# Clustered attention with two feed-forward layers: two instructions that fold the attention output are moved within a hand-written order

## The chip, the cores and the metric

The kernel runs on one core of a Trainium2 chip. The metric is the device time of one execution in microseconds (us); before the change the median of three runs is 757.99 us. Engines are named as in the profile: PE (TensorE matmul), PEld (its weight loads), DVE (VectorE), ACT (ScalarE), POOL (GpSimd) and SP (SyncE, which issues all DMAs here).

## The reference, cut to what matters

Sixteen heads (2 batches of 8) of 768 rows and 64 columns go through attention in which a row sees only the columns of its own cluster; the cluster of a row is the centroid with the largest product. Two dense layers follow, on 1536 rows.

```python
q_assign = argmax(q_n @ c_n.T); k_assign = argmax(k_n @ c_n.T)
scores = where(q_assign[:, None] == k_assign[None, :], q @ k.T / 8, -1e9)
attn = exp(scores - max(scores)); attn = attn / (sum(attn) + 1e-9)
x = attn @ v                                  # heads side by side: 1536 x 512
h = x @ w_in;  x = maximum(0.01 * h, h) @ w_out
h = x @ w_in2; x = maximum(h, 0) ** 2 @ w_out2
```

## The kernel before, in words

Attention takes the first third of the time. It works on 8 pairs of heads, each pair in 6 **units** (3 for each head) of 256 query rows, 48 units in all. A unit u is taken through a pipeline several steps deep; the loop at L712 makes step after step, and in each step it issues the operations that one string of `PLAN` (L21 to L46) lists, in that order. `X0:0` in step u means the first exponential of unit u, `Va:3` means part a of the product with v of unit u-3, `S1:-1` the second score tile of unit u+1. An item with `@` belongs to the preparation of the next pair. Step s below is the step that uses string s, so steps 0 to 5 make up a pair. The order of each engine is exactly the order of the strings (`manual_schedule`, L524) for PE, DVE, ACT and POOL, up to unit 41; from step 42 on (L718) a planner that works from estimated costs and priorities places the instructions of these four engines, until the feed-forward part takes up a hand-written order again. SP's order is always that of the program.

The operations of one unit, with their engine:

- S0, S1 (PE, L389): scores of 128 rows each into a PSUM tile S; two such tiles exist, one for the even and one for the odd half. In steps 5 and 0 some of them also carry the cluster products of the next pair (L297) in the rest of the tile.
- R0, R1 (DVE, L412): row maximum of S. X0, X1 (ACT, L422): exponential of S, with the row sums.
- RE (ACT, L433) adds a small constant to the two row sums; RC (DVE, L436) takes their reciprocal; N0, N1 (POOL, L439) multiply the exponentials by it.
- Ta, Tb, Tc (PE, L452): transposes into a PSUM tile T, of which three exist. Ha, Hb, Hc (ACT, L463) and La, Lb, Lc (DVE, L469) copy T out as a high and a low part, eh and el.
- Va, Vb, Vc (PE, L487): products of eh and el with v, accumulated in the PSUM tile A, of which one exists. Va of a unit therefore needs the unit before to be out of A.
- **FC** (ACT, `fold_a`, L500) copies one half of A's partitions into xt; **FA** (DVE, `fold_b`, L509) adds the other half to it. So FA needs FC, and FC needs Vc.

The preparation of the next pair that matters here: M0, M1 and M2 (DVE, L318 and L319) read the cluster products out of the S tiles in step 0. Then come `desc` (POOL, L324), `m2` (DVE, L330, one reduction in step 1), `oh` (POOL, L337 and L339, the one-hot rows, issued in step 2 ahead of N0 and N1), and `oT` (PE, L350, three transposes of the one-hot rows, step 2 behind Vc). They run so for the pairs 2 to 7, that is six times; the first two pairs are prepared otherwise. `FIRST` selects the same six strings for the first pair.

In both kernels an order list says what each engine does; what an instruction waits for is derived from the tiles, in the order of the program.

```python
    def fold_a(u):
        ...
        nc.scalar.copy(
            out=xt_t[p][64 * j : 64 * j + 64, c : c + 256], in_=a_t[u][64 - 64 * j : 128 - 64 * j]
        )
    def fold_b(u):
        ...
        nc.vector.tensor_tensor(out=x, in0=a_t.pop(u)[64 * j : 64 * j + 64], in1=x, op=ALU.add)
```

Of the kernel before, what the change touches and what calls it, by code (L numbers as in the profile page):

```python
# [19 lines left out]

PLAN = (  # L21
    (
        "ldq@0 Ta:2 X0:0 FA:4 RC:1 Va:3 khi@0 Hc:3 M0@0 Ha:2 R1:0 M1@0 Lc:3 S0:-1 Tb:2 X1:0 "
        "Vb:3 Hb:2 La:2 RE:0 Vc:3 klo@0 N0:1 R0:-1 M2@0 Lb:2 N1:1 S1:-1 FC:3 Tc:2"
    ),
    (
        "Ta:2 qhi@0 qlo@0 X0:0 FA:4 RC:1 Va:3 Hc:3 Ha:2 desc@0 R1:0 Lc:3 S0:-1 Tb:2 X1:0 "
        "Vb:3 Hb:2 La:2 RE:0 Vc:3 N0:1 R0:-1 Lb:2 m2@0 N1:1 S1:-1 FC:3 Tc:2"
    ),
    (  # L30
        "Ta:2 X0:0 FA:4 pl00@0 RC:1 Va:3 Hc:3 oh@0 Ha:2 R1:0 Lc:3 S0:-1 Tb:2 X1:0 Vb:3 "
        "pl10@0 Hb:2 La:2 RE:0 Vc:3 oT@0 N0:1 R0:-1 Lb:2 N1:1 S1:-1 FC:3 Tc:2"
    ),
    (
        "Ta:2 X0:0 FA:4 RC:1 st@0 Va:3 Hc:3 Ha:2 R1:0 Lc:3 S0:-1 Tb:2 X1:0 Vb:3 "
        "pl01@0 Hb:2 vhi@0 La:2 RE:0 Vc:3 N0:1 R0:-1 Lb:2 xhi@0 N1:1 S1:-1 FC:3 Tc:2"
    ),
    (
        "Ta:2 X0:0 FA:4 RC:1 Va:3 xlo@0 Hc:3 Ha:2 R1:0 Lc:3 S0:-1 Tb:2 X1:0 Vb:3 Hb:2 La:2 "
        "RE:0 Vc:3 N0:1 R0:-1 Lb:2 N1:1 S1:-1 FC:3 Tc:2"  # L40
    ),
    (
        "Ta:2 X0:0 FA:4 RC:1 scale@1 vlo@0 ldv@0 Va:3 Hc:3 Ha:2 R1:0 Lc:3 S0:-1 Tb:2 X1:0 "
        "Vb:3 Hb:2 pl11@0 La:2 RE:0 Vc:3 N0:1 R0:-1 Lb:2 N1:1 S1:-1 FC:3 Tc:2"
    ),
)  # L46
FILL = (0,0,1)
# [1114 lines left out]
```

## Time and profile before

| | |
|---|---|
| median of 3 runs | 757.99 us (757.71 to 758.62) |
| the profiled execution's own time | 756.92 us |
| its span in the profile | 755.1 us |
| busy: PE, PEld, DVE, ACT, POOL | 98%, 86%, 76%, 59%, 51% of the span |
| granted TensorE clock | full in all 40 slices of the span |
| DMA | 66.35 MB, mean 88 GB/s |

The span is what the trace covers, from its first to its last instruction; 1.8 us of the execution lie around it. Busy shares are means over an attention part and a feed-forward part that look different: in the attention part DVE, ACT and POOL are nearly as full as PE. A busy PE is one that has a matmul in flight. In the timelines below each row gives a start, a duration, the engine, the source line, the operation and, in brackets, how long the engine stood idle before it and what ended that.

### The profile page before, as it was taken

To read this page: it belongs to the slowest core of one execution; us is meant where nothing else is said; L and a number is where in the kernel's file an instruction comes from. 1 tells how busy PE (TensorE), PEld (TensorE's weight loads), DVE (VectorE), ACT (ScalarE), POOL (GpSimd) and SP (SyncE) were. 2 spreads that over 40 slices of the span, in tenths; PEclk is the share of its full clock that TensorE was granted. 3 is DMA by queue.
4 is the path that set the end of the run, shared out by engine and by line. 5 is a ranking of instruction groups with operands and counts; after the bars stand their busy time and mean duration, and the time that the engine had idled before them with its cause. 6 is when DMAs were issued, how large, how long until landed. Compare 5 with 4: busy or idle time off the path is not lost.

```text
span 755.1 us, 11072 instructions
## 1 busy us (share of the span) xinstructions
PE 743.5 (98%) x4054; PEld 647.8 (86%) x4054; DVE 573.5 (76%) x860; ACT 442.1 (59%) x816; POOL 387.1 (51%) x345
## 2 busy tenths in 40 slices
PE   8999999999999999999999999999999999999997
PEld 8899999999989888888888888888788888888886
DVE  5999999999999545776666566686868677686755
ACT  6988988988998564345353354547644345444430
POOL 2989889889855316461432414399342341423400
PEclk9999999999999999999999999999999999999999
DMA  7493573572601213111131111311112211121004
GB/s 232 106 224 107 116 176 109 116 173 68 151 27 61 109 56 112 56 56 57 56 112 56 56 56 56 111 57 56 56 57 77 90 57 56 56 89 79 1 1 167
DMA packets 16903, 66.35 MB, mean 88 GB/s; under 512 B 3153, under 2 KB 4049, under 8 KB 11857
## 3 DMA queue, kind: packets, MB, share of 16 engines
q1 hardware_dynamic: 16848, 65.65, 29.2%
q8 instruction: 32, 0.52, 0.3%
q14 instruction: 23, 0.18, 0.1%
HBM read 44.60 MB, written 3.15 MB: 63 GB/s over the span
## 4 chain that ended last, share of the span: by engine, by line
PE 83%; DVE 11%; ACT 5%; issue 1%; POOL 0%; DVEq 0%; ACTq 0%; POOLq 0%
PE o L848 34%; PE h L770 31%; PE A L487 6%; PE S L389 5%; PE T L452 5%; DVE el L469 3%; DVE nm L412 3%; ACT e L422 2%; DVE xt L509 1%; ACT eh L463 1%; DVE xl L1008 1%; DVE ds L319 1%; DVE m L318 1%; PE warm L242 1%; PE S L297 1%
## 5 line engine op out<-in xcount | busy, mean ns | idle before, releaser
L134 POOL TENSOR_TENSOR wl<-wt,wh 128x1024 fp32r<-128x1024 f32 x32 | 76.9, 2403 | 130.7 <-ACT wh L133 130.7
L819 DVE TENSOR_TENSOR gl<-h,gh 128x512 fp32r<-128x512 f32 x96 | 65.7, 690 | 68.9 <-ACT h L814 50.2
L770 PE MATMUL h<-xl,wh 128*128 128x512 f32 x288 | 112.2, 390 | 0.0
L770 PE MATMUL h<-xh,wh 128*128 128x512 f32 x288 | 111.8, 390 | 0.1
L770 PE MATMUL h<-xh,wl 128*128 128x512 f32 x288 | 111.9, 389 | 0.0
L866 DVE TENSOR_TENSOR acc<-o,acc 128x512 f32<-128x512 f32 x144 | 92.9, 686 | 12.4 <-PE o L848 12.4
L469 DVE TENSOR_TENSOR el<-T,eh 128x512 fp32r<-128x512 f32 x144 | 94.4, 683 | 4.4 <-ACT eh L463 3.2
L439 POOL TENSOR_SCALAR e<-e,r 128x768 f32<-128x768 f32 x96 | 87.4, 922 | 18.3 <-DVE r L436 12.1
L412 DVE TENSOR_REDUCE nm<-S 128x1 f32<-128x768 f32 x96 | 90.9, 948 | 4.7 <-PE S L297 2.4
L422 ACT ACTIVATE e<-S,nm 128x768 f32<-128x768 f32 x96 | 87.2, 909 | 11.0 <-DVE nm L412 6.8
L389 PE MATMUL S<-hb 128*128 128x384 f32 (+1 forms) x384 | 90.2, 349 | 1.6 <-ACT e L422 1.2
L463 ACT CAST eh<-T 128x512 fp32r<-128x512 f32 x144 | 79.8, 589 | 13.5 <-PE T L452 13.2
L487 PE MATMUL A<-eh,vv 128*128 128x256 f32 x288 | 79.6, 306 | 2.0 <-DVE xt L509 2.0
L452 PE MATMUL T<-ident,e 128*128 128x128 f32 x576 | 79.6, 273 | 1.0 <-DVE el L469 1.0
L848 PE MATMUL o<-gl,wh 128*128 128x512 f32 x192 | 74.8, 390 | 0.0
L197 POOL TENSOR_TENSOR ws<-wt 128x256 f32<-128x256 f32 x24 | 17.8, 740 | 111.1 <-DVE wt L173 111.1
L848 PE MATMUL o<-gh,wl 128*128 128x512 f32 x192 | 74.7, 389 | 0.0
L848 PE MATMUL o<-wh,gh 128*128 128x512 f32 x192 | 74.7, 389 | 0.0
L848 PE MATMUL o<-wh,gl 128*128 128x512 f32 x192 | 74.7, 389 | 0.0
L848 PE MATMUL o<-wl,gh 128*128 128x512 f32 x192 | 74.7, 389 | 0.0
L848 PE MATMUL o<-gh,wh 128*128 128x512 f32 x192 | 73.6, 389 | 0.0
L487 PE MATMUL A<-el,vv 128*128 128x256 f32 x288 | 72.5, 282 | 0.3 <-DVE el L469 0.3
(136 smaller groups left out, 1600.9 us busy)
## 6 DMA issues: line engine op xcount, KB each, us to landing
wraw<-w SPq DMA_DIRECT2D x32, 1024.0 KB, 4.7
hb<-spl SPq DMA_DIRECT2D x14, 576.0 KB, 4.6
hb<-spl SPq DMA_DIRECT2D x42, 192.0 KB, 5.1
rqk<-qk SPq DMA_DIRECT2D x16, 384.0 KB, 3.8
rv<-v SPq DMA_DIRECT2D x8, 384.0 KB, 3.3
out<-q SPq DMA_DIRECT2D x12, 256.0 KB, 2.0
twice<-qk SPq DMA_DIRECT2D x8, 192.0 KB, 5.9
hb<-st SPq DMA_DIRECT2D x56, 24.0 KB, 1.9
```

Of the source, the lines that this page charges most:

```text
L134: return lambda: nc.gpsimd.tensor_tensor(out=wl, in0=t, in1=wh.bitcast(F32), op=ALU.subtract)
L389: nc.tensor.matmul(out=s[:, c, 0:HALF], lhsT=hb[0:k, a, i * 128 : (i + 1) * 128], rhs=hb[0:k, b, c * HALF : (c + 1) * HALF], start=(a == 0 ...
L412: nc.vector.tensor_reduce(out=n, in_=s_t[t][:, :, 0:HALF], axis=AX.XY, op=ALU.max, negate=True)
L422: nc.scalar.activation(out=e.rearrange("p (a b) -> p a b", a=2), in_=s_t.pop(t)[:, :, 0:HALF], func=AF.Exp, bias=n_t.pop(t), scale=1.0, ac ...
L439: nc.gpsimd.tensor_scalar(out=e_t[t], in0=e_t[t], scalar1=r_t[t // 2][:, t % 2 : t % 2 + 1], scalar2=1.0, op0=ALU.mult, op1=ALU.mult,)
L452: nc.tensor.transpose(T[:, o : o + 128], e_t[2 * u + b][:, kc * 128 : (kc + 1) * 128], ident)
L463: nc.scalar.copy(out=eh[:, 2 * g : 2 * g + 2, :].rearrange("p a b -> p (a b)"), in_=T_t[u, g])
L469: nc.vector.tensor_tensor(out=el[:, 2 * g : 2 * g + 2, :].rearrange("p a b -> p (a b)"), in0=T_t.pop((u, g)), in1=eh[:, 2 * g : 2 * g + 2, ...
L487: nc.tensor.matmul(out=A, lhsT=w, rhs=m[:, kc, :], start=(kc == 0 and i == 0), stop=(kc == KC - 1 and i == 1),)
L770: nc.tensor.matmul(out=out, lhsT=l, rhs=r, start=(first and i == 0), stop=(i == n - 1), skip_group_check=not first,)
L848: nc.tensor.matmul(out=outs[o], lhsT=l, rhs=r, start=(first and i == 0), stop=(last and i == 2),)
L866: nc.vector.tensor_tensor(out=a, in0=ps, in1=a, op=ALU.add)
```

## The change

Only `PLAN` changes, in the same way in its six strings. FC goes from behind S1 to right behind Vc. FA was the second DVE instruction of the step after (lag 4); it becomes lag 3, behind R0 and ahead of Lb. RC goes from behind FA (lag 1) to right behind R0 of its own step (lag 0), ahead of FA. In string 0 this pair of instructions comes ahead of M2 as well. Two of the six strings:

```diff
-        "ldq@0 Ta:2 X0:0 FA:4 RC:1 Va:3 khi@0 Hc:3 M0@0 Ha:2 R1:0 M1@0 Lc:3 S0:-1 Tb:2 X1:0 "
-        "Vb:3 Hb:2 La:2 RE:0 Vc:3 klo@0 N0:1 R0:-1 M2@0 Lb:2 N1:1 S1:-1 FC:3 Tc:2"
+        "ldq@0 Ta:2 X0:0 Va:3 khi@0 Hc:3 M0@0 Ha:2 R1:0 M1@0 Lc:3 S0:-1 Tb:2 X1:0 "
+        "Vb:3 Hb:2 La:2 RE:0 Vc:3 FC:3 klo@0 N0:1 R0:-1 RC:0 FA:3 M2@0 Lb:2 N1:1 S1:-1 Tc:2"
...
-        "Ta:2 qhi@0 qlo@0 X0:0 FA:4 RC:1 Va:3 Hc:3 Ha:2 desc@0 R1:0 Lc:3 S0:-1 Tb:2 X1:0 "
-        "Vb:3 Hb:2 La:2 RE:0 Vc:3 N0:1 R0:-1 Lb:2 m2@0 N1:1 S1:-1 FC:3 Tc:2"
+        "Ta:2 qhi@0 qlo@0 X0:0 Va:3 Hc:3 Ha:2 desc@0 R1:0 Lc:3 S0:-1 Tb:2 X1:0 "
+        "Vb:3 Hb:2 La:2 RE:0 Vc:3 FC:3 N0:1 R0:-1 RC:0 FA:3 Lb:2 m2@0 N1:1 S1:-1 Tc:2"
```

## Rows read from the trace of the kernel before

**Rows 1.** Page: the span, and PE's busy time, share and instructions.

```profile
span 755.1 us, 11072 instructions
...
PE 743.5 (98%) x4054; PEld 647.8 (86%) x4054; DVE 573.5 (76%) x860; ACT 442.1 (59%) x816; POOL 387.1 (51%) x345
```

**Rows 2.** Busy time of each engine in one pair, from step 2 to step 2.

```profile
137.79:166.19 28.40, 28.06 (x220) 27.43 (x220) 26.82 (x50) 24.50 (x57) 25.29 (x25) 1.00 0.55 133
```

**Rows 3.** Waits of PE's weight loads, 14 to 262 us: total, times, longest.

```profile
PEld A L487 <- DVE xt L509: 3.5, 6, 0.6
...
PEld T L452 <- POOL e L439: 1.3, 1, 1.3
```

**Rows 4.** Timeline of DVE, steps 4 to 1 of a pair, up to step 2.

```profile
148.30 0.95 DVE L412 TENSOR_REDUCE nm<-S 128x1 f32<-128x768 f32 x1
...
155.65 0.29 DVE L318 TENSOR_REDUCE m<-S 128x8 f32<-128x128 f32 x1 [0.53 <-ACT e L422]
...
158.84 0.95 DVE L412 TENSOR_REDUCE nm<-S 128x1 f32<-128x768 f32 x1
159.70 0.28 DVE L318 TENSOR_REDUCE m<-S 128x8 f32<-128x128 f32 x1
160.02 0.29 DVE L319 TENSOR_TENSOR ds<-S,m 128x128 f32<-128x128 f32 x1
160.23 0.68 DVE L469 TENSOR_TENSOR el<-T,eh 128x512 fp32r<-128x512 f32 x1
...
161.60 0.96 DVE L412 TENSOR_REDUCE nm<-S 128x1 f32<-128x768 f32 x1
...
164.53 0.68 DVE L469 TENSOR_TENSOR el<-T,eh 128x512 fp32r<-128x512 f32 x1
165.13 0.55 DVE L330 TENSOR_REDUCE m<-ds 128x24 f32<-128x384 f32 x1
165.71 0.43 DVE L509 TENSOR_TENSOR xt<-A,xt 64x256 f32<-64x256 f32 x1
```

**Rows 5.** Timeline of ACT, steps 4, 0 and 1.

```profile
149.23 0.37 ACT L500 COPY xt<-A 64x256 f32<-64x256 f32 x1
...
157.82 0.90 ACT L422 ACTIVATE e<-S,nm 128x768 f32<-128x768 f32 x1 [0.52 <-DVE ds L319]
...
159.61 0.30 ACT L433 ACTIVATE r<-r,eps 128x2 f32<-128x2 f32 x1
160.08 0.36 ACT L500 COPY xt<-A 64x256 f32<-64x256 f32 x1 [0.17 <-PE A L487]
160.47 0.90 ACT L422 ACTIVATE e<-S,nm 128x768 f32<-128x768 f32 x1
...
162.65 0.90 ACT L422 ACTIVATE e<-S,nm 128x768 f32<-128x768 f32 x1 [0.23 <-DVE nm L412]
...
164.33 0.36 ACT L500 COPY xt<-A 64x256 f32<-64x256 f32 x1
```

**Rows 6.** Timeline of PE, steps 1 and 2.

```profile
162.00 0.88 PE L389 MATMUL S<-hb 128*128 128x384 f32 x4
...
164.81 1.04 PE L452 MATMUL T<-ident,e 128*128 128x128 f32 x8
166.19 0.39 PE L487 MATMUL A<-eh,vv 128*128 128x256 f32 x1 [0.34 <-DVE xt L509]
...
168.87 0.34 PE L350 MATMUL ohT<-identb,oh 128*128 128x128 bf16 x3
...
169.82 1.04 PE L452 MATMUL T<-ident,e 128*128 128x128 f32 x8
170.61 0.36 PE L487 MATMUL A<-eh,vv 128*128 128x256 f32 x1
```

**Rows 7.** Timeline of POOL, step 2: one-hot rows, then N0 and N1.

```profile
166.69 1.49 POOL L339 TENSOR_SCALAR oh<-ds 128x384 bf16<-128x384 f32 x1
168.16 1.79 POOL L439 TENSOR_SCALAR e<-e,r 128x768 f32<-128x768 f32 x2
```

More of the change, by code (lines that the diff above doesn't have):

```diff
@@ L22 @@
     (
-        "ldq@0 Ta:2 X0:0 FA:4 RC:1 Va:3 khi@0 Hc:3 M0@0 Ha:2 R1:0 M1@0 Lc:3 S0:-1 Tb:2 X1:0 "
-        "Vb:3 Hb:2 La:2 RE:0 Vc:3 klo@0 N0:1 R0:-1 M2@0 Lb:2 N1:1 S1:-1 FC:3 Tc:2"
-    ),
-    (
-        "Ta:2 qhi@0 qlo@0 X0:0 FA:4 RC:1 Va:3 Hc:3 Ha:2 desc@0 R1:0 Lc:3 S0:-1 Tb:2 X1:0 "
-        "Vb:3 Hb:2 La:2 RE:0 Vc:3 N0:1 R0:-1 Lb:2 m2@0 N1:1 S1:-1 FC:3 Tc:2"
-    ),
-    (
-        "Ta:2 X0:0 FA:4 pl00@0 RC:1 Va:3 Hc:3 oh@0 Ha:2 R1:0 Lc:3 S0:-1 Tb:2 X1:0 Vb:3 "
-        "pl10@0 Hb:2 La:2 RE:0 Vc:3 oT@0 N0:1 R0:-1 Lb:2 N1:1 S1:-1 FC:3 Tc:2"
-    ),
-    (
-        "Ta:2 X0:0 FA:4 RC:1 st@0 Va:3 Hc:3 Ha:2 R1:0 Lc:3 S0:-1 Tb:2 X1:0 Vb:3 "
-        "pl01@0 Hb:2 vhi@0 La:2 RE:0 Vc:3 N0:1 R0:-1 Lb:2 xhi@0 N1:1 S1:-1 FC:3 Tc:2"
-    ),
-    (
-        "Ta:2 X0:0 FA:4 RC:1 Va:3 xlo@0 Hc:3 Ha:2 R1:0 Lc:3 S0:-1 Tb:2 X1:0 Vb:3 Hb:2 La:2 "
-        "RE:0 Vc:3 N0:1 R0:-1 Lb:2 N1:1 S1:-1 FC:3 Tc:2"
-    ),
-    (
-        "Ta:2 X0:0 FA:4 RC:1 scale@1 vlo@0 ldv@0 Va:3 Hc:3 Ha:2 R1:0 Lc:3 S0:-1 Tb:2 X1:0 "
-        "Vb:3 Hb:2 pl11@0 La:2 RE:0 Vc:3 N0:1 R0:-1 Lb:2 N1:1 S1:-1 FC:3 Tc:2"
+        "ldq@0 Ta:2 X0:0 Va:3 khi@0 Hc:3 M0@0 Ha:2 R1:0 M1@0 Lc:3 S0:-1 Tb:2 X1:0 "
+        "Vb:3 Hb:2 La:2 RE:0 Vc:3 FC:3 klo@0 N0:1 R0:-1 RC:0 FA:3 M2@0 Lb:2 N1:1 S1:-1 Tc:2"
+    ),
+    (
+        "Ta:2 qhi@0 qlo@0 X0:0 Va:3 Hc:3 Ha:2 desc@0 R1:0 Lc:3 S0:-1 Tb:2 X1:0 "
+        "Vb:3 Hb:2 La:2 RE:0 Vc:3 FC:3 N0:1 R0:-1 RC:0 FA:3 Lb:2 m2@0 N1:1 S1:-1 Tc:2"
+    ),
+    (
+        "Ta:2 X0:0 pl00@0 Va:3 Hc:3 oh@0 Ha:2 R1:0 Lc:3 S0:-1 Tb:2 X1:0 Vb:3 "
+        "pl10@0 Hb:2 La:2 RE:0 Vc:3 FC:3 oT@0 N0:1 R0:-1 RC:0 FA:3 Lb:2 N1:1 S1:-1 Tc:2"
+    ),
+    (
+        "Ta:2 X0:0 st@0 Va:3 Hc:3 Ha:2 R1:0 Lc:3 S0:-1 Tb:2 X1:0 Vb:3 "
+        "pl01@0 Hb:2 vhi@0 La:2 RE:0 Vc:3 FC:3 N0:1 R0:-1 RC:0 FA:3 Lb:2 xhi@0 N1:1 S1:-1 Tc:2"
+    ),
+    (
+        "Ta:2 X0:0 Va:3 xlo@0 Hc:3 Ha:2 R1:0 Lc:3 S0:-1 Tb:2 X1:0 Vb:3 Hb:2 La:2 "
+        "RE:0 Vc:3 FC:3 N0:1 R0:-1 RC:0 FA:3 Lb:2 N1:1 S1:-1 Tc:2"
+    ),
+    (
+        "Ta:2 X0:0 scale@1 vlo@0 ldv@0 Va:3 Hc:3 Ha:2 R1:0 Lc:3 S0:-1 Tb:2 X1:0 "
+        "Vb:3 Hb:2 pl11@0 La:2 RE:0 Vc:3 FC:3 N0:1 R0:-1 RC:0 FA:3 Lb:2 N1:1 S1:-1 Tc:2"
     ),
```

## The prediction

> **What bounds the kernel now.** I read the page first: PE is busy for 98% of the span [rows 1], so the change can win only what PE loses to waits, and every new wait of PE adds to the time. The change touches the attention part alone, so the next view is the busy time of one whole pair of heads there [rows 2]: 28.40 us, of which PE is busy 28.06 and DVE 26.82. The reader is to see that both are nearly full; DVE has only some 1.6 us to give in a pair. The third view, the waits of the weight loads, says what PE waits for: six times, 0.6 us each, Va waits for FA [rows 3]. The fourth is PE's timeline, for the place and the full size of it: in step 2 of a pair, Va starts 1.38 us after the first of the eight transposes ahead of it, where the same eight take 0.79 us one step later [rows 6]. So one wait costs 0.59 us, and six make the 3.5 us of the list. The fifth is DVE's timeline [rows 4]: FA at 165.71 stands directly behind m2 (165.13), and m2 behind Lb (164.53). FA is late because DVE is behind, not because A is late: FC had ended at 164.69 [rows 5]. DVE is behind from step 0 on, where M0 to M2 are added; from M0 at 155.65 up to FA no row of DVE in that stretch shows an idle bracket.
>
> **FC: nothing.** ACT issues nothing between the old and the new place of FC in any of the six strings, so its order is the same. FC still waits for Vc.
>
> **FA and RC: the old wait goes.** In step 1, FA moves ahead of Lb and m2. That takes 0.6 us of Lb (from 164.53 to 165.13) and the 0.55 us of m2 out of its way, and PE's 0.59 us wait goes: a gain of 0.59 per pair. None of the moved instructions issues a DMA, and POOL's and SP's orders stay; RC ready earlier only lets N0 start earlier.
>
> **FA: the new wait.** Where FA now stands it can meet an FC that has not ended. Its neighbours in the queue, Lb, M2 and m2, then wait with it, and what needs these. Plain step first: R0 starts at 148.30 and the next DVE instruction follows 0.86 later, as behind R0 at 158.84 [rows 4], so RC and FA would be due from 149.16 on, but FC ends at 149.60 [rows 5]. DVE loses 0.4 us once per pair there; later plain steps meet FC already late by as much. It is hidden, since DVE idles 0.53 us ahead of M0, which waits for an exponential on ACT [rows 4]. Step 0 then starts M0 at the same point relative to PE.
>
> Step 0, in the times of rows 4 to 7:
> - R0 at 158.84 is followed at 159.70. RC needs RE, which ends at 159.91. FA needs FC, which ends at 160.44; it starts at 160.47 (X0 follows FC by 0.03 on ACT; I take the same) and lasts 0.43. M2, at 159.70 before, comes at 160.93, **1.23 us late**. Its second half ended at 160.31 and now ends at 161.54.
> - X0 of step 1 reads the S tile that M2 reads. The kernel keeps such reads apart, in program order: M0 waited for an exponential [rows 4], and X1 at 157.82 waited 0.52 us for M1's second half [rows 5]. So X0 moves from 160.47 to about 161.64 and ends at 162.54. S0 of step 1 needs that tile back; it ran at 162.00 [rows 6] and now at about 162.60. **PE waits 0.60 us**, as long as it used to wait for FA.
>
> Step 1:
> - From X0 to FC took 3.86 us on ACT, 0.23 of it idle ahead of X1 [rows 5], which the lateness fills. FC comes at 161.64 + 3.63 = 165.27 and ends at 165.63; FA runs from 165.66 to 166.09. DVE is there by then: its R0 would have to be more than 1.1 us late to miss that (its successor came at 164.53), and it is some 0.7 us late. Va of step 2 is due at 164.81 + 0.79 + 0.60 = 166.20 and finds FA done.
> - Lb follows at 166.12 and m2 at 166.72, **1.59 us late**, with PE at the very point where it was before.
>
> Step 2: `oh` needs m2, and N0 and N1 stand behind `oh` on POOL. Before, they ended at 169.95 [rows 7], and the first of the transposes Ta, which need them, was due at 169.82 + 0.40 = 170.22: 0.27 us of slack. Now they end at 171.54, and Ta waits until about 171.58: **PE loses 1.36 us**, of which some 0.9 are lost already ahead of oT, which needs `oh` (168.18 before, 168.87 on PE). In these 1.4 us DVE catches up, and steps 3 to 5 run as before.
>
> **The sum.** Per pair: 0.60 + 1.36 - 0.59 = 1.37 us more; six pairs, 8.2 us. Before and after these six I take nothing: the first pair has no M0 to M2, m2 or oT in the strings. The last pair is placed by the planner, whose order the profile of before can't tell; its bounds are a gain of the 1.3 us that a weight load waited there for POOL [rows 3] and a loss of the plain 0.4 us in each of six steps, 2.4 us. The profiled execution took 756.92 us, its span 755.1 and 1.8 around it; 8.2 more is 765.1. The median is 1.07 us above that execution, so 766.2 us. The price that no row shows is how soon FA follows FC and Ta follows N1, and how much of DVE's own delay adds to it: I bound the 1.37 by 1.05 and 1.45 (0.3 less if ACT runs more closely than in its 3.63 us, 0.1 more for three hand-overs), 764.3 to 766.7 before the last pair's bounds.
>
> **The rivals.**
> - *The wait goes and nothing takes its place.* Faster: six times 0.59, 3.5 us, 754.5 us. It decides at one point: FC must have ended when DVE has finished R0 and RC. For it: FC's end at 164.69 lies near the point at which DVE was through with R0 in step 1 (164.53). Against it: in step 0 it ends at 160.44, 0.74 us behind the 159.70 at which DVE is ready, and the plain step shows 0.4. The row says first that PE's gap ends with FA; the Trainium skill, Perfetto Trace Analysis, section Optimization Strategy, advises just such a step: find the gap of the limiting engine, find what it waits for, and make that start sooner. By that rule the result would be this rival's; the trace agrees with it on the gap and not on what stands behind it in DVE's queue. Chance 0.11.
> - *One wait for another.* The new 0.60 us at S0 takes the place of the old 0.59, and m2's lateness ends in slack: 758.0 us. That needs m2 less than 0.27 us late against PE [rows 6, 7]; worked out, it is 1.59. Chance 0.06.
> - *X0 isn't held by M2.* Then only DVE's own delay counts. In step 0 behind FA come M2's 0.53 us and Lb's 0.6, so R1 of step 1 moves from 161.60 to 162.06, 0.46 late. R0's successor moves from 164.53 to 164.99, and RC and FA (0.5) put Lb at 165.5 and m2 at 166.1, 0.97 late. N1 ends at 170.92, Ta was due at 170.22 - 0.59 = 169.63: 1.3 lost, 0.59 won, 0.7 per pair, 762.2 us. Against it stand the two waits between readers of one tile. Chance 0.09.
>
> **How the numbers follow.** A measurement of this kernel tells a change from none from about 0.2%, 1.5 us. My forecast has 0.74. Slower takes it and the third rival, 0.83; the same takes the second, 0.06; faster the first, 0.11. The range reaches from 760.5, the third rival with the planner's gain, to 769.0, the upper bound with the planner's loss; it leaves out the first two rivals, 0.17.
>
> **What the profile of after would show.** Right: no Va waits for FA in step 2; FA has ACT's copy as releaser in every pair, with some 0.5 us of idle time in step 0; S0 of step 1 waits for an exponential, six times, near 0.6 us; the transposes of step 2 wait for POOL or DVE, six times, near 1.4 us with oT's part; a pair takes about 29.8 us. Wrong: if the pair takes 27.8 us, FA doesn't wait in step 0. If S0 doesn't wait, M2 doesn't hold X0. If oT and Ta don't wait, one-hot rows have slack that I don't see.

## The result and the profile after

The changed kernel takes 766.69 us (median of 4 runs, 765.63 to 767.49) against 757.85 us before (4 runs): a ratio of 1.0113, 95% interval 1.0101 to 1.0125, or 8.8 us slower. The prediction was 766.2 us.

First the page of the kernel after, its span and the line of PE, then the busy time of one pair of heads, between two equal points of step 1 (the stretch, its length, the busy time of PE, PEld, DVE, ACT and POOL, the granted clock, the busy share of DMA and its GB/s), and the waits of PE's weight loads from 14 to 275 us (total, times, longest).

```profile
span 765.7 us, 11062 instructions
...
PE 747.0 (98%) x4054; PEld 648.3 (85%) x4054; DVE 575.0 (75%) x860; ACT 443.6 (58%) x816; POOL 386.5 (50%) x345
```

```profile
139.22:168.93 29.71, 28.47 (x220) 27.47 (x220) 27.02 (x50) 24.74 (x56) 25.22 (x25) 1.00 0.53 128
```

```profile
PEld S L389 <- ACT e L422: 7.9, 12, 1.4
PEld L350 <- POOL oh L339: 3.8, 6, 0.6
PEld T L452 <- POOL e L439: 2.6, 6, 0.4
```

Against [rows 2] a pair takes 29.71 instead of 28.40 us, 1.31 more, while the engines are busy for nearly as long as before. So the time went into waits. The wait of Va for FA [rows 3] is gone from the list altogether. (FA was the first DVE instruction of its step before the change, not the second, as the section on the change has it.) Three waits stand in its place, each of them in six pairs: S0 for an exponential (12 times in the list, 6 of them in the pairs), oT for the one-hot rows on POOL, and Ta, which the list puts down to N1 on POOL. The Ta meant here is the first item of string 3; it follows Tc of step 2 directly. Before the change the list had S0's wait only outside the pairs:

```profile
PEld S L389 <- ACT e L422: 2.5, 6, 1.4
```

Where they come from is read from DVE's timeline, step 0 to the start of step 2, of the pair that lies some 6 us later in this profile:

```profile
165.07 0.95 DVE L412 TENSOR_REDUCE nm<-S 128x1 f32<-128x768 f32 x1
166.18 0.17 DVE L436 RECIPROCAL r<-r 128x2 f32<-128x2 f32 x1 [0.16 <-ACT r L433]
166.71 0.43 DVE L509 TENSOR_TENSOR xt<-A,xt 64x256 f32<-64x256 f32 x1 [0.37 <-ACT xt L500]
167.17 0.29 DVE L318 TENSOR_REDUCE m<-S 128x8 f32<-128x128 f32 x1
167.50 0.29 DVE L319 TENSOR_TENSOR ds<-S,m 128x128 f32<-128x128 f32 x1
167.71 0.68 DVE L469 TENSOR_TENSOR el<-T,eh 128x512 fp32r<-128x512 f32 x1
...
171.82 0.43 DVE L509 TENSOR_TENSOR xt<-A,xt 64x256 f32<-64x256 f32 x1 [0.15 <-ACT xt L500]
172.28 0.69 DVE L469 TENSOR_TENSOR el<-T,eh 128x512 fp32r<-128x512 f32 x1
172.89 0.54 DVE L330 TENSOR_REDUCE m<-ds 128x24 f32<-128x384 f32 x1
```

R0 of step 0 starts at 165.07. Before, M2 followed it 0.86 us later [rows 4]; now RC waits for RE, FA waits for FC, and M2 starts 2.10 us behind R0. That is 1.24 us late. ACT's timeline of the same pair shows who waits for M2:

```profile
166.32 0.36 ACT L500 COPY xt<-A 64x256 f32<-64x256 f32 x1 [0.17 <-PE A L487]
167.88 0.90 ACT L422 ACTIVATE e<-S,nm 128x768 f32<-128x768 f32 x1 [1.20 <-DVE ds L319]
```

X0 of step 1 used to follow FC directly [rows 5]; now ACT stands idle for 1.20 us between them, until M2's second half (167.50 + 0.29 = 167.79) has ended. PE's timeline has the consequences:

```profile
168.93 0.98 PE L389 MATMUL S<-hb 128*128 128x384 f32 x4 [0.59 <-ACT e L422]
...
171.84 1.04 PE L452 MATMUL T<-ident,e 128*128 128x128 f32 x8
172.63 0.36 PE L487 MATMUL A<-eh,vv 128*128 128x256 f32 x1
...
176.00 0.34 PE L350 MATMUL ohT<-identb,oh 128*128 128x128 bf16 x3 [0.42 <-POOL oh L339]
...
176.95 0.60 PE L452 MATMUL T<-ident,e 128*128 128x128 f32 x4
177.77 0.63 PE L452 MATMUL T<-ident,e 128*128 128x128 f32 x4 [0.22 <-POOL e L439]
178.15 0.36 PE L487 MATMUL A<-eh,vv 128*128 128x256 f32 x1
```

A reader should not take the brackets for the price here: a matmul row lasts past the start of the next, so the bracket is shorter than the delay. Delays are read from starts. Va of step 2 now follows its eight transposes by 0.79 us (171.84 to 172.63) instead of 1.38 [rows 6]. From Va of step 2 to Va of step 3 PE takes 5.52 us instead of 4.42 [rows 6], so step 2 loses 1.10. S0 of step 1 is about 0.75 late: the product ahead of it starts at 168.06, four such products follow each other at 0.12, and it starts at 168.93. Together 0.75 + 1.10 - 0.59 = 1.26 of the 1.31.

POOL's timeline shows the chain from m2 to the one-hot rows and N1, and DVE's the Lb of step 2:

```profile
173.52 0.84 POOL L337 TENSOR_TENSOR ds<-ds,m 128x384 f32<-128x384 f32 x1 [2.87 <-DVE m L330]
174.45 1.49 POOL L339 TENSOR_SCALAR oh<-ds 128x384 bf16<-128x384 f32 x1
175.92 1.78 POOL L439 TENSOR_SCALAR e<-e,r 128x768 f32<-128x768 f32 x2
```

```profile
176.93 0.69 DVE L469 TENSOR_TENSOR el<-T,eh 128x512 fp32r<-128x512 f32 x1
```

oT starts 0.06 us behind the one-hot rows (174.45 + 1.49 = 175.94). The four transposes of Tc start at 176.95; at the pace of eight in 0.79 us Ta would be due at about 177.35, and it starts at 177.77. N1 ends at 177.70, Lb at 177.62. The bracket names POOL, but two things speak for Lb as what Ta's first transpose waited for: that transpose reads only the tile that N0 has multiplied (the loop in `trans`, L452, takes the unit's two row tiles in turn), and its start lies 0.15 us behind Lb's end, just as in two kernels below in which N1 had ended 1.30 us (M2 and m2 ahead) and 0.62 us (FA moved in step 1 alone) before Ta. Why Ta needs Lb is told with the second experiment.

From Va of unit 0 to Va of unit 36, which takes in the six pairs, PE needs 170.81 us before (28.20 to 199.01) and 178.51 after (29.35 to 207.86): 7.7 of the 8.8 us. By the medians the last 1.1 lies outside them. In the two profiled executions, whose spans are 10.6 us apart, the first score product starts 1.1 later, and from Va of unit 36 to the end of the span it is 557.8 us instead of 556.1. A part of this is seen as far as Va of unit 42, where the planner has taken over, before and after:

```profile
199.01:226.77 27.76, 26.43 (x200) 25.16 (x198) 27.32 (x46) 26.19 (x57) 18.50 (x18) 1.00 0.18 54
207.86:236.25 28.39, 26.52 (x200) 25.03 (x198) 27.26 (x45) 25.97 (x56) 17.88 (x18) 1.00 0.16 49
```

These 0.6 us are taken up by two of the experiments; the rest is not located.

### The profile page after: what moved, and what is told of

It reads as the page before. It is cut to its first block, busy times and chain, and to the rows that moved or that the text cites. A ratio compares the mean times of both kernels' runs of the same rounds, so it can differ in the third digit from the quotient of the medians.

```text
span 765.7 us, 11062 instructions
## 1 busy us (share of the span) xinstructions
PE 747.0 (98%) x4054; PEld 648.3 (85%) x4054; DVE 575.0 (75%) x860; ACT 443.6 (58%) x816; POOL 386.5 (50%) x345
## 4 chain that ended last, share of the span: by engine, by line
PE 81%; ACT 7%; DVE 6%; POOL 2%; DMA 1%; issue 1%; SPq 0%; DVEq 0%; ACTq 0%
PE o L848 32%; PE h L770 30%; PE A L487 6%; PE T L452 5%; PE S L389 5%; ACT e L422 3%; PE S L297 2%; POOL e L439 1%; DVE el L469 1%; ACT eh L463 1%; DVE xt L509 1%; DVE xl L1008 1%; DMA rqk<-qk 1%; POOL ds L337 1%; ACT xt L500 1%
## 5 line engine op out<-in xcount | busy, mean ns | idle before, releaser
L452 PE MATMUL T<-ident,e 128*128 128x128 f32 x576 | 81.0, 274 | 2.5 <-POOL e L439 1.3
L452 PEld LDWEIGHTS T<-ident,e 128*128 128x128 f32 x576 | 68.8, 144 | 7.1 <-POOL e L439 2.6
```

The lines of the kernel that those rows point to most:

```text
L452: nc.tensor.transpose(T[:, o : o + 128], e_t[2 * u + b][:, kc * 128 : (kc + 1) * 128], ident)
```

## The experiments

The theory: an FA that waits for FC holds up what stands behind it in DVE's queue. In step 0 this is M2, which holds X0 and so S0; in step 1 it is m2, whose lateness reaches oT and Ta through POOL. The rivals: RC's wait for RE is the cause; X0 isn't held by M2, and DVE's lateness alone counts; FA costs DVE time wherever it stands a step earlier; and the planner's part carries the loss. All kernels were timed beside the kernel before, whose medians were then 757.83 to 758.09 us.

**M2 ahead of RC and FA** (from the changed kernel, string 0):

```diff
- R0:-1 RC:0 FA:3 M2@0 Lb:2
+ R0:-1 M2@0 RC:0 FA:3 Lb:2
```

> The changed kernel with M2 ahead of RC and FA in string 0, nothing else. Theory (FA, waiting for FC, holds up M2, and M2 holds X0): S0 of step 1 no longer waits for the exponential (0.80 us per pair on the weight loads after the change, now under 0.1), X0 of step 1 starts as early as before the change; but m2 is still late behind FA in step 1, so the transposes of step 2 still wait; a pair falls from 29.7 to 28.6 to 28.9 us, the time to 760 to 763 us. Rival (M2 doesn't hold X0, the lateness is DVE's own): S0 goes on waiting, the pair stays within 0.2 of 29.7 us, the time at 766.

762.27 us, ratio to before 1.0057 (1.0042 to 1.0072). S0 has no wait any more in the six pairs, a pair takes 28.80 us, and X0 of step 1 follows FC directly again. The waits of oT and Ta are left:

```profile
143.01:171.81 28.80, 28.14 (x219) 27.40 (x220) 26.78 (x50) 24.87 (x56) 25.29 (x25) 1.00 0.54 131
```

```profile
171.81 0.17 PEld L350 LDWEIGHTS <-oh 128*128 128x128 bf16 x3 [0.63 <-POOL oh L339]
173.56 0.42 PEld L452 LDWEIGHTS T<-ident,e 128*128 128x128 f32 x4 [0.44 <-POOL e L439]
```

```profile
163.05 0.36 ACT L500 COPY xt<-A 64x256 f32<-64x256 f32 x1 [0.17 <-PE A L487]
163.44 0.90 ACT L422 ACTIVATE e<-S,nm 128x768 f32<-128x768 f32 x1
```

One exchange gives back 0.9 of 1.3 us a pair. That M2 holds X0 is shown: nothing else that X0 needs was moved.

**M2 and m2 ahead** (the same, and string 1):

```diff
- R0:-1 RC:0 FA:3 Lb:2 m2@0
+ R0:-1 m2@0 RC:0 FA:3 Lb:2
```

> As the kernel with M2 ahead, and m2 ahead of RC and FA in string 1 too. Theory (the one-hot chain m2, oh, N0, N1 is what makes step 2 lose): oT no longer waits for POOL (0.63 us per pair after the change, now under 0.1), and the wait of Ta in step 2 for POOL goes; a pair falls below that of the kernel with M2 ahead if nothing else holds Ta. Rival (Ta is held by the third T tile, which Lb of step 2, behind FA, gives back): Ta waits for DVE instead, 0.6 to 1.0 us, and the pair stays at 28.6 us, the time near 760 us.

760.94 us, 1.0041 (1.0026 to 1.0056); a pair takes 28.78 us. The wait of oT is gone, as the theory has it, but the pair gains nothing: Ta of step 2 still waits, now for DVE. That was the rival of this run, and it is right. PE's timeline, and DVE's:

```profile
171.54 0.60 PE L452 MATMUL T<-ident,e 128*128 128x128 f32 x4
172.92 0.63 PE L452 MATMUL T<-ident,e 128*128 128x128 f32 x4 [0.78 <-DVE el L469]
```

```profile
171.62 0.43 DVE L509 TENSOR_TENSOR xt<-A,xt 64x256 f32<-64x256 f32 x1
172.08 0.69 DVE L469 TENSOR_TENSOR el<-T,eh 128x512 fp32r<-128x512 f32 x1
```

Lb of step 2 ends at 172.77, and Ta of the next unit starts at 172.92. There are three T tiles, and the three transposes of one-hot rows take one out of turn, so that this Ta gets the tile that Lb has just left. With FA ahead of Lb the tile comes back later. The same hold is there in the changed kernel: Lb ends 0.15 us ahead of Ta there too. So step 2 is held in two ways that run side by side, by POOL and by the T tile, and either is enough. Without Va's old wait a pair would take about 28.40 - 0.59 = 27.81 us; the T tile alone makes it 28.78 (this kernel), POOL alone 28.73 (m2 alone late, below), both 28.80 (M2 ahead, above).

**RC back at its old place**, FA alone behind R0 (all six strings):

```diff
- Ta:2 X0:0 ... R0:-1 RC:0 FA:3
+ Ta:2 X0:0 RC:1 ... R0:-1 FA:3
```

> The changed kernel with RC back at its old place at the start of the next step (FA alone behind R0). Theory (FA's wait for FC is the cause, RC's wait for RE lies inside it): a pair stays at 29.6 to 29.7 us, FA still waits for ACT's copy, the time is 765.5 to 767. Rival (RC, which now waits for RE in its own step, is the cause): a pair comes back to 28.4 to 28.7 us, the time to 758 to 761.

766.74 us, 1.0121 (1.0104 to 1.0138): the time of the changed kernel, and its pair. RC isn't the cause.

```profile
138.40:168.16 29.76, 28.53 (x219) 27.47 (x220) 26.55 (x50) 24.76 (x56) 25.32 (x25) 1.00 0.53 126
```

**RC and FA moved in step 0 alone** (from the kernel before):

```diff
- (string 0) R0:-1 M2@0 Lb:2 N1:1 S1:-1 FC:3 Tc:2
+ (string 0) FC:3 klo@0 N0:1 R0:-1 RC:0 FA:3 M2@0 Lb:2 N1:1 S1:-1 Tc:2
- (string 1) X0:0 FA:4 RC:1 Va:3
+ (string 1) X0:0 Va:3
```

> The kernel before with RC and FA moved in step 0 alone, ahead of M2 and Lb. Theory (step 0 carries the start of the loss): S0 of step 1 waits for the exponential, 0.7 to 0.8 us, though FA of step 1 stays at its old place; Va of step 2 goes on waiting for FA; a pair takes 28.9 to 29.3 us, the time is 761 to 764 us. Rival (step 0 is harmless alone, the loss comes from FA ahead of m2 in step 1): 28.4 us and 758.

762.05 us, 1.0053 (1.0036 to 1.007), a pair 29.10 us. The new wait stands beside the old one:

```profile
166.39 0.65 PEld L389 LDWEIGHTS S<-hb 128*128 128x128 f32 x4 [0.79 <-ACT e L422]
170.57 0.19 PEld L487 LDWEIGHTS A<-eh,vv 128*128 128x128 f32 x1 [0.47 <-DVE xt L509]
```

Six times 29.10 - 28.40 is 4.2 us, and the kernel is 4.2 us slower than before. Here the pairs carry all of it, and the waits behind the sixth pair are those of the kernel before. S0's wait needs nothing but step 0's RC and FA ahead of M2, and RC is ruled out above.

**m2 alone late** (from the kernel before; FA and FC stay where they were):

```diff
- (string 1) R0:-1 Lb:2 m2@0 N1:1
+ (string 1) R0:-1 Lb:2 N1:1
- (string 2) X0:0 FA:4 pl00@0 RC:1 Va:3
+ (string 2) X0:0 FA:4 pl00@0 RC:1 m2@0 Va:3
```

> The kernel before with m2 alone moved, from the end of step 1 to step 2 behind FA and RC, so 0.8 to 1.0 us later; FA stays where it was and meets no FC that is late. Theory (a late m2 costs PE by itself, through the one-hot rows on POOL and the multiplications behind them): Va of step 2 no longer waits for FA (0.58 us gained), oT and Ta wait for POOL, about 1.0 us together, and a pair takes 28.7 to 29.0 us, the time is 759.5 to 762. Rival (the one-hot rows have slack, what cost the changed kernel was DVE's waiting for FC): a pair takes 27.8 to 28.0 us, the time is 754.5 to 756.

761.33 us, 1.0043 (1.0028 to 1.0058), a pair 28.73 us. No Va waits for FA in the six pairs, and yet the pair is 0.33 longer:

```profile
170.83 0.17 PEld L350 LDWEIGHTS <-oh 128*128 128x128 bf16 x3 [0.51 <-POOL oh L339]
172.59 0.31 PEld L452 LDWEIGHTS T<-ident,e 128*128 128x128 f32 x3 [0.35 <-POOL e L439]
```

So a late m2 costs PE by itself, without any wait for FC: the second half of the theory. Here Ta's first transpose went ahead and the other three waited (x3 in the row), so N1 holds Ta only from its second transpose on. Six times 0.33 is 2.0 of the 3.5 us; the rest lies outside the six pairs.

**Lb ahead of RC and FA in all strings but string 1** (from the kernel with M2 and m2 ahead):

```diff
- R0:-1 M2@0 RC:0 FA:3 Lb:2
+ R0:-1 M2@0 Lb:2 RC:0 FA:3
- R0:-1 RC:0 FA:3 Lb:2
+ R0:-1 Lb:2 RC:0 FA:3
```

> The kernel with M2 and m2 ahead, and Lb ahead of RC and FA in all strings but string 1. Theory (an FA that waits costs only what stands behind it in DVE's queue; the wait of Ta in step 2 was the T tile that Lb gives back late): the wait of Ta shrinks from 0.99 to about 0.3 us, Va of step 2 doesn't wait, a pair takes 28.0 to 28.2 us, less than the 28.41 of before, the time is 755 to 757.5 us. Rival (FA's lag itself, a step earlier, costs DVE time wherever it stands): a pair stays at 28.7 to 28.9 us, the time at 760 to 761.

A pair takes 28.25 us and Ta's wait is 0.32, so the rival (FA costs DVE time wherever it stands) falls:

```profile
143.57:171.82 28.25, 28.14 (x219) 27.44 (x220) 26.65 (x50) 24.50 (x56) 25.25 (x25) 1.00 0.56 134
```

But the time is 758.39 us, 1.0008 (0.9999 to 1.0017), not below 757.5: the six pairs' gain of 0.9 us was lost outside them. In its profile the stretch from Va of unit 36 to the end is 558.0 us, where the kernel before has 556.1.

**FA moved in step 1 alone, with m2 ahead** (from the kernel before):

```diff
- (string 1) Vc:3 N0:1 R0:-1 Lb:2 m2@0 N1:1 S1:-1 FC:3 Tc:2
+ (string 1) Vc:3 FC:3 N0:1 R0:-1 m2@0 FA:3 Lb:2 N1:1 S1:-1 Tc:2
- (string 2) X0:0 FA:4 pl00@0 RC:1
+ (string 2) X0:0 pl00@0 RC:1
```

> The kernel before with FA moved in step 1 alone, ahead of Lb, with m2 ahead of it. Theory: Va of step 2 no longer waits for FA (0.58 us before), and Ta a little for Lb of step 2: a pair takes 28.1 to 28.2 us, the time is 755.5 to 757 us. Rival (DVE is full, so PE can't gain at all): 28.4 us and 758.

The shortest pair of all, 28.18 us, as expected:

```profile
141.66:169.84 28.18, 28.04 (x219) 27.45 (x219) 26.65 (x50) 24.48 (x56) 25.30 (x25) 1.00 0.56 134
```

The time was a miss: 758.63 us, 1.001 (1.0001 to 1.0019). Of the 0.59 us that Va had waited, a wait of Ta took back 0.36; the rest of the gain, 1.3 us in six pairs, is gone in the whole. The stretch from Va of unit 36 to the end is 557.2 us in its profile against 556.1, which accounts for 1.1 of it.

**The planner's part.** Two kernels cross the orders at step 42, where the planner begins. In step 42 an FA and an RC are left out or put in, so that every unit has each of them once. One has the changed order up to step 41 and the strings of before from there:

> The changed order up to step 41 and the strings of before from step 42 on, which is the part that the planner places. If the six pairs carry all of the loss: the time is that of the changed kernel, 766 to 767 us. If the planner's part has lost about 1 to 1.7 us, as the two traces read after the sixth pair: 765 to 765.7, with the waits of transposes at the end of attention like those of before.

The other is the reverse:

> The strings of before up to step 41, the new ones from step 42 on, the part that the planner places. If the new strings themselves cost time there: 758.6 to 760 us with new waits after the sixth pair. If the planner's result hangs on what comes before it and not on the strings: like the kernel before, 757.5 to 758.5 us, with the waits of before (a transpose behind POOL, about 1.3 us).

The first takes 767.45 us, 1.0129 (1.0114 to 1.0144): nothing of what was lost behind the pairs comes back, and neither of its two cases names that. The second takes 757.49 us, 0.9996 (0.9987 to 1.0005), like before. Weight loads behind the sixth pair that waited, first of the changed kernel, then of the first kernel, then of the second (the line numbers of these two are higher by 26):

```profile
225.93 0.66 PEld L389 LDWEIGHTS S<-hb 128*128 128x128 f32 x4 [0.87 <-ACT e L422]
228.02 0.19 PEld L487 LDWEIGHTS A<-el,vv 128*128 128x128 f32 x1 [0.23 <-DVE el L469]
230.13 0.42 PEld L452 LDWEIGHTS T<-ident,e 128*128 128x128 f32 x4 [0.67 <-issue]
```

```profile
226.35 0.66 PEld L415 LDWEIGHTS S<-hb 128*128 128x128 f32 x4 [0.88 <-ACT e L448]
228.43 0.19 PEld L513 LDWEIGHTS A<-el,vv 128*128 128x128 f32 x1 [0.23 <-DVE el L495]
230.54 0.42 PEld L478 LDWEIGHTS T<-ident,e 128*128 128x128 f32 x4 [0.67 <-issue]
```

```profile
219.90 0.19 PEld L513 LDWEIGHTS A<-el,vv 128*128 128x128 f32 x1 [0.55 <-DVE el L495]
222.62 0.43 PEld L478 LDWEIGHTS T<-ident,e 128*128 128x128 f32 x4 [1.27 <-POOL e L465]
```

The old strings give the changed kernel's waits and the new strings give those of before [rows 3]. From Va of unit 36 to Va of unit 42 the first takes 28.39 us, like the changed kernel, the second 27.75, like the kernel before. In the traces PE's 4054 matmuls stand in the same order, by their tiles, in the first as in the changed kernel and in the second as in the kernel before. So what the planner makes of the last pair hangs on the order that stands ahead of it, not on the strings that it is handed. Which of its estimates tips over was not tried.

**A later start of the planner** (from the kernel with FA moved in step 1 alone; step 44, shown here, then step 43, in place of step 42):

```diff
- if u == NU - 6:
+ if u == NU - 4:
      manual.close()
```

> The kernel with FA moved in step 1 alone (a pair of 28.18 us), with the hand-written order kept two steps longer, up to step 43. If its six pairs' gain of 1.4 us was lost because the planner placed the last pair otherwise, and a later start of the planner places it as well as before: 756 to 757 us. If the planner does no better from there: 758 to 760 us.

> The same with the hand-written order kept one step longer, up to step 42: 756 to 757 us if the place of the planner's start decides, 758 to 760 if not.

757.65 us, 0.9994 (0.9983 to 1.0004), and 757.74 us, 0.9995 (0.9985 to 1.0005), with pairs of 28.20 and 28.18 us. Both times lie between the two cases of their expectations: less is lost than with the planner's start at step 42, but the result can't be told from the kernel before. No version beat it clear of the noise.

## Why the prediction was right, step by step

The sign and the place of each wait were right, and so was the mechanism up to oT; what holds Ta behind it was only half seen. The terms compare like this.

- *The old wait goes*: 0.59 us a pair predicted, and the 0.79 us from the eight transposes to Va now say the same.
- *M2 late by 1.23 us in step 0*: 1.24 in the trace. The hand-over taken from ACT, FA 0.03 behind FC's end, is that of the rows (166.32 + 0.36 = 166.68, FA at 166.71).
- *S0 waits 0.60 us*: about 0.75. The undersized piece is the hand-over from X0 to S0, taken as 0.06 where the rows show 0.15 (X0 ends at 168.78, S0 starts at 168.93), and X0 itself starts 0.26 behind Va of step 1 (167.62), where the sum had 0.22.
- *m2 late, so Ta loses 1.36 us*: 1.10. Against Va of step 2, m2 moved from 1.06 us ahead of it [rows 4, 6] to 0.26 us behind (172.89 against 172.63), which is 1.32 where the sum had 1.58. PE's longer wait at S0 gave 0.15 of that back, and ACT needs 3.55 from X0 to FC (167.88 to 171.43), not 3.63. The path is right as far as oT. Behind it the prediction has the first transpose of Ta wait for N1; by the runs N1 holds only the second, and the T tile that Lb gives back late ends about when N1 does.
- *The sum*: 1.37 a pair predicted, 1.31 measured. It came out well since the two errors have opposite signs; 1.31 lies within the stated 1.05 to 1.45.
- *The last pair: nothing*, with bounds of -1.3 and +2.4. What lies outside the six pairs lost about 1.1 by the medians, 0.6 of it seen between Va of unit 36 and Va of unit 42. The bounds held. What I could not have read from the profile of before is that the planner's result depends on the order ahead of it.

The rivals: that the wait goes and nothing takes its place failed at the point that was named for it, since FC's end comes after DVE has finished R0 in step 0. That X0 isn't held by M2 failed by the run with M2 ahead. That one wait just replaces another was half right: S0's wait is about as long as FA's was, but m2's lateness didn't end in slack. The Trainium skill (Perfetto Trace Analysis, section Optimization Strategy) advises to find the gaps of the limiting engine and to make what it waits for start sooner or end faster. The runs bear that out where what is put behind loses less than the wait that goes: moved in step 1 alone, with m2 ahead of it, FA shortens the pair by 0.22 us, though not the whole kernel; moved as in the change, it lengthens the pair by 1.31.

One thing was missed: the third T tile as a second reason for Ta to wait. That the sum came out all the same is luck, since this hold costs as much as POOL's (28.78 against 28.73 us a pair) and ends at about the same time. Had the one-hot rows had slack, as the second rival needs, the pair would still have lost: so it did with m2 ahead, which made the hold visible.

Two slips in the working don't touch the sum. The lower end of the range, the third rival's 762.2 less the planner's 1.3, is 760.9 and not 760.5. And that rival takes 0.5 us for RC and FA, where the kernel after shows 0.66 from RC's start to Lb's (176.27 to 176.93).

## What to carry to other kernels

Before an instruction is moved earlier in an in-order queue, look at when its own input ends against the time at which the queue would reach it, and price the wait by what stands behind it, not by what waited for it before. When the engine that takes the wait is nearly as full as the bounding one (here 26.8 against 28.1 us of a pair), an idle half microsecond in it comes back as a wait of the bounding engine, even two engines further on. A short reader of a shared PSUM tile can be the dearest thing to delay, if a longer reader is ordered behind it. And where a wait that a profile names is taken away and nothing is gained, look for a second one beside it, as the T tile beside POOL here.

## What the runs showed of the hardware that was not expected

The time from FA's start to the next start on DVE depends on the half of the partitions that it reads and writes. Two FAs of the changed kernel, both followed by Lb: for a unit of the first head of a pair (partitions 0 to 63 of xt) it is 0.34 us, for the second head (64 to 127) 0.46 us. The profile's durations, 0.42 and 0.43 to the digit shown, don't tell it. In the traces of before and after, the other FAs of the hand-written part that have no wait behind them lie within 0.02 us of these two values.

```profile
160.87 0.42 DVE L509 TENSOR_TENSOR xt<-A,xt 64x256 f32<-64x256 f32 x1 [0.37 <-ACT xt L500]
161.21 0.67 DVE L469 TENSOR_TENSOR el<-T,eh 128x512 fp32r<-128x512 f32 x1
...
176.47 0.43 DVE L509 TENSOR_TENSOR xt<-A,xt 64x256 f32<-64x256 f32 x1
176.93 0.69 DVE L469 TENSOR_TENSOR el<-T,eh 128x512 fp32r<-128x512 f32 x1
```

Why was not tried. The start of the kernel also varies from profile to profile, whatever the order: the first score product starts at 13.2 us before, 14.25 after and between 13.3 and 14.8 in the experiments, which is why totals were compared by their medians and pairs by their own spans.
